# RWKV-6 attention and a SiLU expert on one core: the first three units in a written order instead of a merged one

## The chip, the cores and the metric

The kernel runs on one core of one Trainium2 chip. The metric is device time in microseconds. Before the change three runs took 745.05, 746.13 and 749.16 us; the median is 746.13.

## The reference

For 4 sequences, 8 heads, 768 steps and 48 channels a head, the attention keeps a 48x48 state for each head:

```python
for t in range(S):
    cur = np.einsum('bhd,bhe->bhde', u[None] * kt, vt)
    y[:, :, t] = np.einsum('bhd,bhde->bhe', rt, state + cur)
    state = wt[:, :, :, None] * state + np.einsum('bhd,bhe->bhde', kt, vt)
...
x = attn_out.transpose(0, 2, 1, 3).reshape(B * S, H * D)
h = x @ w_in
out = ((h * (1.0 / (1.0 + np.exp(-h)))) @ w_out).astype(np.float32)
```

r, k, v, w and u are float32. w_in (384x2048) and w_out (2048x384) are float64, so the kernel must also turn the weights into float32.

## The kernel before

**Units.** The work is cut into 12 units: 6 chunks of 128 steps times 2 pairs of sequences. In a unit, `b` is 0 or 1 for the sequence of the pair; the second one is stored in reversed order of time. Heads lie in pairs: 4 pairs (NP) for each sequence, 8 (Q) in all, and a head takes 64 partitions, 48 of them filled.

**Attention of a unit.** `turn` (L287) brings w, r and k from tokens-on-partitions to channels-on-partitions. In units 0 and 1 (NTOK) this is done by TensorE (L307) with an evacuation by ScalarE (L308); from unit 2 on the data comes in blocks of 32 (`load_blocks`, L89, four DMAs each) and VectorE transposes it (L298). Then seven levels follow (`level`, L353). In level l, blocks of 2^l steps are joined in pairs: ScalarE copies the untouched half of the keys for the next level (L365), TensorE forms scores of the later block's queries against the earlier block's keys (L377, 16 recorded matmuls), VectorE keeps the ones that belong to this level under a mask (L386, two instructions), VectorE multiplies the later queries by a product of w (L395), and POOL multiplies half of the keys (L414, two instructions). The level products of w come from POOL (L322): unit 0 makes one in each level, later units all seven at once (`products`). Unit 0 multiplies the queries before it keeps the scores; later units keep first.

`bonus` (L331) makes r·k·u for the diagonal on POOL (L333, L334), `bonus_sum` (L336) sums it on VectorE (L340) and copies the second sequence's part on ScalarE (L343), `bonus_write` (L345) writes it into the diagonal of the scores (L347, L349). `reverse_v` (L315) reverses the values of the second sequence in place (L317). `y_state` and `y` (L437, L445) form the output of the unit on TensorE, `dense_x` (units 0 and 1, L483) or `move_x` (DMAs, L495) packs it into xt; `turn_k` (L422) and `update` (L459, L475) carry the state on. `clear` (L313) zeroes padding of a raw buffer before blocks are loaded into it.

**Keys.** The tile `tk` has 16 rows of 128 for each partition. Rows 0 to 7 hold the keys of the unit, rows 8 to 11 and 12 to 15 the keys that even and odd levels read (`x_at`). The key products of L414 write in one instruction both into the keys and into the rows that the next level reads, with a step between them.

**Expert.** `up(i, m)` (L549) multiplies two 128-column blocks of w_in with the unit's xt and ScalarE applies Silu (L552) into a `gt` buffer; there are eight `up` in a unit. `down` (unit 0, L559, eight parts) and `quarter` (later units, L604, seven quarters, a scheme with seven products in place of eight) multiply with w_out. The quarters need `sums` of gt (L586) and `weight_sums` of w_out (L578), made by VectorE.

**Weights.** They come as 16 pieces. `load_weight` (L151) brings the 64-bit words of a piece into a staging place, either one of three `own` places or a part of w_out_sb that isn't filled yet; `PLACES` says which, and a place that was used before is loaded again only after the earlier piece is joined (`due`). `round_weight(i)` (L203) issues the addition of what is joined so far (POOL, L201), joins piece i-1 (VectorE, L189 and L191, each twice), splits piece i (VectorE L169; ScalarE L173 twice, L175) and issues the loads that are now due. The buffers `temps` hold two pieces, so a split waits for the addition of the piece two before it. The tails of a split lie in the two `p_o` banks.

**Order.** Every engine runs its instructions in the order in which the program issues them. `mix(i)` gives a unit's attention steps with shares, `merge` (L634) sorts several lists of steps by shares over given stretches and issues them. Units 0 to 2 are one merge of 12 lists (L652); from unit 3 on a unit's attention is merged with `quarter`s of unit i-2 and `up`s of unit i-1 (L657). Set-up (L214 to L279) comes ahead of all: memsets on VectorE, the identity, masks and the diagonal mask `own_mask` on POOL, the first loads on SP.

Of the kernel before, what the change touches and what calls it, by code (L numbers as in the profile page):

```python
# [33 lines left out]
def kernel(  # L34
# [11 lines left out]
    nc = tc.nc  # L46
# [9 lines left out]
    NX = Q + 2 * NP  # L56
    TU = NB * L
# [74 lines left out]
    PLACES = [3, 4, 5, 6, 0, 1, 2, 3, 4, 5, 6, 0, 1, 2, 6, 0]  # L132
# [81 lines left out]
    for s in range(NSLOT):  # L214
        nc.vector.memset(raw[:, s].rearrange("p x b h d -> p (x b h) d")[:, :, D:PD], 0.0)
# [22 lines left out]
    nc.vector.memset(state, 0.0)  # L238
# [36 lines left out]
    own_mask = const.tile([128, NB, L], I8, name="own_mask")  # L275
    nc.gpsimd.memset(own_mask, 1)
    for b, sign in ((0, 1), (1, -1)):
        nc.gpsimd.affine_select(out=own_mask[:, b], in_=own_mask[:, b], compare_op=ALU.is_equal, fill=0.0,
                                base=-b * (L - 1), pattern=[[1, L]], channel_multiplier=-sign)  # L279


# [5 lines left out]
    def turn(i, b, name):  # L287
        dst = {"w": tw, "r": tr, "k": tk}[name]
        if b == 0:
            rows = NX if name == "k" else Q  # L290
            t = pt.tile([128, rows, L], F32, name="t" + name, bufs=1)
            dst[i] = [t] if name == "w" else t
        t = dst[i][0] if name == "w" else dst[i]
        to, back = t[:, b * NP:(b + 1) * NP, :], name == "k" and b == 1
        if i < NTOK:
            turn_all(i, b, name, to, back)
        else:
            nc.vector.transpose(out=to[:, ::-1, ::-1] if back else to,  # L298
                                in_=raw[:, i % NSLOT, WRK[name], b].rearrange("p h d -> p (h d)"))
# [9 lines left out]

    def clear(i):  # L310

        room = raw[:, i % NSLOT].rearrange("p x b h d -> p (x b h d)").rearrange("p (g d) -> p g d", d=32)[:, :, D - 32:32]
        nc.scalar.copy(out=room, in_=zero[:, :, None].to_broadcast([128, room.shape[1], room.shape[2]]))  # L313
# [17 lines left out]
    def bonus(i, b):  # L331
        ruk[i, b] = pt.tile([128, H, D], F32, name="ruk")
        nc.gpsimd.tensor_tensor(out=ruk[i, b], in0=rk(i, b, 0), in1=rk(i, b, 1), op=ALU.mult)  # L333
        nc.gpsimd.tensor_tensor(out=ruk[i, b], in0=ruk[i, b], in1=u_bc, op=ALU.mult)  # L334

    def bonus_sum(i, b):  # L336
        if b == 0:
            diag[i] = pt.tile([128, NB, H], F32, name="diag", bufs=2)
        to = pt.tile([128, H], F32, name="diag_b") if b == 1 else diag[i][:, 0]
        nc.vector.tensor_reduce(out=to, in_=ruk[i, b], axis=mybir.AxisListType.X, op=ALU.add)  # L340
        if b == 1:
            for g in range(4):
                nc.scalar.copy(out=diag[i][(3 - g) * 32:(4 - g) * 32, 1], in_=to[g * 32:(g + 1) * 32])  # L343
# [9 lines left out]
    def level(i, l):  # L353
# [3 lines left out]
        x_at, next_at = Q + l % 2 * NP, Q + (l + 1) % 2 * NP  # L357
# [5 lines left out]
        if l + 1 < NL:  # L363

            nc.scalar.copy(out=keys(next_at * L + c, [4 * c, NP * ni // 2], [c, 2], [1, c]),  # L365
                           in_=keys(c, [4 * c, NP * ni // 2], [NP * L + c, 2], [1, c]))
# [33 lines left out]
        for b in range(NB):  # L400
            if l + 1 < NL:
                start = [next_at * L, b * NP * L][b] + b * c
                step = 2 * c + (1 - 2 * b) * (b * NP - next_at) * L
# [3 lines left out]
            else:  # L407
                out = keys(b * NP * L + b * c, [L, NP], [1, c])
# [93 lines left out]
    def mix(i):  # L502

        steps = []
        for name in ("krw", "wrk")[i] if i < NTOK else "wkr":

            steps += [((1, 0.3)[i] if i < NTOK else 0, turn, i, b, name) for b in range(NB)]
            if name == "w" and i > 0:
                steps.append((0, products, i))
        if i >= NTOK:  # L510
            steps.append((TURNS, lambda: None))
        steps.append((0, reverse_v, i))
        for l in range(NL):
# [7 lines left out]
        turns = [(1 if i > 0 else 0.3, turn_k, i, b) for b in range(NB)]  # L521
        ys = [(0, y_state, i, b) for b in range(NB)] + [(0, y, i, b) for b in range(NB)]
        updates = [(0, update, i, b) for b in range(NB)]
        if i < NTOK:
            steps += ys + [(0, dense_x, i, b) for b in range(NB)] + turns + updates
        else:
            steps += turns + ys + updates + [(1, move_x, i)]

        last = [at for at, step in enumerate(steps) if step[1] is (bonus if i < NTOK else turn)][-1] + 1
        loads = block_loads(i + NSLOT) if NTOK <= i and i + NSLOT < len(units) else []  # L530
        if 2 <= i + 1 < len(units):
# [6 lines left out]
        steps = spread  # L538
        return steps


    gt, po = {}, {}

    def up(i, m):
# [6 lines left out]
        gt[i, m] = pt.tile([128, 2, TU], F32, name="gt", bufs=FC // 2 + 3)  # L551
# [94 lines left out]
    def early_blocks(i):  # L646
        return [(1, *step) for step in [(clear, i - NSLOT)] + [step[1:] for step in block_loads(i)]]
# [40 lines left out]
```

## Time and profile before

| What | Value |
|---|---|
| median of the three runs | 746.13 us |
| the profiled execution's own time | 745.98 us |
| its span, from first to last instruction | 744.3 us |
| PE busy | 681.8 us (92%) |
| DVE (VectorE) busy | 441.1 us (59%) |
| POOL busy | 270.9 us (36%) |
| ACT (ScalarE) busy | 174.7 us (23%) |
| mean granted TensorE clock | 0.956 |

In the page's slices each digit is the busy share of one fortieth of the span, 18.6 us, in tenths, and PEclk is the granted TensorE clock in tenths of full speed. In the table by stretches, each engine has its busy microseconds and the number of instructions, then follow the granted clock, the share of time in which the DMA engines were busy, and GB/s. A row of the timeline has start, duration, engine, line, operation, output and inputs, and in brackets how long the engine had been idle and what ended that. PEld is the loading of matmul weights, which overlaps PE. SPq and ACTq are DMA issues. Rows of DMA issues give the number, the size and the median time from issue to landing.

### The profile page before, as it was taken

The page shows a single profiled execution, that of the slowest core. Times are in us where ns is not written, and L with a number is a line of the kernel's source. Part 1 is how long each engine was busy: PE and PEld are TensorE (multiplying, and loading weights), DVE is VectorE, ACT ScalarE, POOL GpSimd, SP SyncE. Part 2 cuts the span into 40 slices and gives each one's busy share as a digit, 9 for nine tenths or more (in the row PEclk, how much of TensorE's full clock was granted, in tenths as well). Part 3 has the DMA queues.
Part 4 walks back from the last instruction along what each step waited for, and adds up shares of the span by engine and source line. Part 5 has one row for each costly group of instructions (what it writes and reads, how often), then busy time and mean ns, then how long its engine had stood idle before and what let it go on. Part 6 is the DMA issues. An engine that isn't in the chain of part 4 may idle for free.

```text
span 744.3 us, 12848 instructions
## 1 busy us (share of the span) xinstructions
PE 681.8 (92%) x4880; PEld 598.5 (80%) x4880; DVE 441.1 (59%) x783; ACT 174.7 (23%) x366; POOL 270.9 (36%) x376
## 2 busy tenths in 40 slices
PE   4584788399999999999999999999999999999998
PEld 3573666257988988988988988988988988988998
DVE  3746695977556656646646646756746747645122
ACT  4243444601202213112112113113112123022020
POOL 8725744570361351441442432431431441330000
PEclk9586789799999999999999999999999999999999
DMA  9904760554225234234144143143143020100000
GB/s 209 268 2 107 167 151 10 110 82 80 44 45 89 39 64 71 39 73 66 33 80 60 33 86 55 34 86 57 29 91 57 19 64 15 41 11 20 24 1 22
DMA packets 224239, 49.04 MB, mean 66 GB/s; under 512 B 212017, under 2 KB 219057, under 8 KB 224177
## 3 DMA queue, kind: packets, MB, share of 16 engines
q1 hardware_dynamic: 224032, 48.02, 33.5%
q8 instruction: 39, 0.64, 0.4%
q10 hardware_dynamic: 144, 0.20, 0.1%
q14 instruction: 24, 0.19, 0.1%
HBM read 39.52 MB, written 4.72 MB: 59 GB/s over the span
## 4 chain that ended last, share of the span: by engine, by line
PE 81%; DVE 9%; POOL 3%; ACT 2%; SPq 2%; issue 2%; DMA 1%; DVEq 0%; POOLq 0%
PE p_h L549 34%; PE p_o L604 24%; PE p_sc L377 11%; DVE score L386 4%; PE p_m L437 3%; PE p_m L445 3%; PE p_o L559 3%; DVE tr L395 2%; POOL tk L414 1%; DVE temps L191 1%; PE p_sc L459 1%; DVE p_o L189 1%; POOL w_in_sb L201 1%; ACT kq L424 1%; PE p_m L483 1%
## 5 line engine op out<-in xcount | busy, mean ns | idle before, releaser
L549 PE MATMUL p_h<-xt,w_in_sb 128*128 128x256 f32 x1152 | 276.7, 395 | 16.1 <-POOL w_in_sb L201 16.1
L549 PEld LDWEIGHTS p_h<-xt,w_in_sb 128*128 128x128 f32 x1152 | 220.8, 196 | 52.1 <-POOL w_in_sb L201 17.1
L386 DVE COPY_PREDICATED score<-mask,p_sc 128x512 f32<-128x512 int8 x162 | 133.4, 889 | 130.5 <-PE p_sc L377 130.5
L414 POOL TENSOR_TENSOR tk<-tk,tw 128x256 f32<-128x256 f32 x168 | 119.0, 730 | 213.1 <-PE p_sc L377 114.4
L552 ACT ACTIVATE gt<-p_h 128x512 f32<-128x512 f32 x96 | 57.1, 595 | 284.2 <-PE p_h L549 284.1
L377 PEld LDWEIGHTS p_sc<-tr,tk 48*128 48x128 f32 x1296 | 84.4, 197 | 48.3 <-issue 25.0
L377 PE MATMUL p_sc<-tr,tk 48*128 48x128 f32 x1296 | 100.2, 296 | 22.2 <-POOL tk L414 12.4
L604 PE MATMUL p_o<-w_out_sb,gt 128*128 128x192 f32 x528 | 90.3, 328 | 0.0
L604 PE MATMUL p_o<-own,temps 128*128 128x192 f32 x528 | 90.0, 328 | 0.0
L604 PEld LDWEIGHTS p_o<-w_out_sb,gt 128*128 128x128 f32 x528 | 86.2, 190 | 1.7
L604 PEld LDWEIGHTS p_o<-own,temps 128*128 128x128 f32 x528 | 85.9, 190 | 1.1
L395 DVE TENSOR_TENSOR tr<-tr,tw 128x512 f32<-128x512 f32 x82 | 65.7, 801 | 3.9 <-POOL ruk L333 2.2
L322 POOL TENSOR_TENSOR tw<-tw 128x512 f32<-128x512 f32 (+6 forms) x84 | 39.4, 468 | 75.3 <-DVE tw L298 66.8
L365 ACT COPY tk<-tk 128x256 f32<-128x256 f32 x72 | 32.7, 454 | 129.8 <-POOL tk L414 85.9
L464 POOL TENSOR_TENSOR state<-state,tw 128x512 f32<-128x512 f32 x16 | 16.3, 1041 | 87.8 <-PE p_m L437 87.8
L586 DVE TENSOR_TENSOR temps<-gt 128x256 f32<-128x256 f32 x88 | 36.9, 419 | 15.6 <-ACT gt L552 15.3
L613 DVE TENSOR_TENSOR ob<-p_o,partial 128x192 f32<-128x192 f32 x44 | 15.5, 352 | 39.5 <-PE p_o L604 39.4
L349 DVE COPY_PREDICATED score<-own_mask,diag 128x1024 f32<-128x1024 int8 x24 | 31.3, 1360 | 0.4
L604 PE MATMUL p_o<-w_out_sb,temps 128*128 128x192 f32 x176 | 31.3, 331 | 0.0
L604 PEld LDWEIGHTS p_o<-w_out_sb,temps 128*128 128x128 f32 x176 | 28.4, 190 | 1.1
L473 DVE TENSOR_TENSOR state<-p_sc,state 48x384 f32<-48x384 f32 x16 | 8.9, 555 | 32.9 <-PE p_sc L459 32.8
L334 POOL TENSOR_TENSOR ruk<-ruk,u_bc 128x384 f32<-128x384 f32 x24 | 26.0, 1081 | 1.9
(83 smaller groups left out, 563.5 us busy)
## 6 DMA issues: line engine op xcount, KB each, us to landing
out_dram<-ob SPq DMA_DIRECT2D x24, 192.0 KB, 1.9
w_out_sb<-in_moe_w_in_dram SPq DMA_DIRECT2D x5, 768.0 KB, 7.0
tokens_rk<-in_r_dram SPq DMA_DIRECT2D x10, 384.0 KB, 4.1
tokens_rk<-in_k_dram SPq DMA_DIRECT2D x10, 384.0 KB, 5.4
w_out_sb<-in_moe_w_out_dram SPq DMA_DIRECT2D x4, 768.0 KB, 4.9
own<-in_moe_w_out_dram SPq DMA_DIRECT2D x4, 768.0 KB, 5.2
xt<-yt SPq DMA_DIRECT2D x60, 48.0 KB, 2.0
raw<-in_w_dram SPq DMA_DIRECT2D x80, 32.0 KB, 2.2
```

The costliest lines, as they stand in the source:

```text
L322: nc.gpsimd.tensor_tensor(out=up, in0=t[:, :, 0::2], in1=t[:, :, 1::2], op=ALU.mult)
L334: nc.gpsimd.tensor_tensor(out=ruk[i, b], in0=ruk[i, b], in1=u_bc, op=ALU.mult)
L349: nc.vector.copy_predicated(out=score[:, i % NSC, e].rearrange("p (b q) t -> p b q t", b=NB), mask=own_mask[:, :, None, :].to_broadcast([1 ...
L365: nc.scalar.copy(out=keys(next_at * L + c, [4 * c, NP * ni // 2], [c, 2], [1, c]), in_=keys(c, [4 * c, NP * ni // 2], [NP * L + c, 2], [1, ...
L377: nc.tensor.matmul(bass.AP(tensor=s_p.tensor, offset=s_p.offset, ap=[s_p.ap[0], [apart * L // 2, 2], [1, L // 2]]), lhsT=tk[i][rows, x_at ...
L386: nc.vector.copy_predicated(out=dst, mask=masks[l][:, :, None].to_broadcast([128, NB, NP, ni, c]), data=sc[e].rearrange("p (b q) (i c) -> ...
L395: nc.vector.tensor_tensor(out=rb[:, :, :, 1, :], in0=rb[:, :, :, 1, :], in1=t[:, :, 0::2][:, :, :, None].to_broadcast([128, Q, ni, c]), op ...
L414: nc.gpsimd.tensor_tensor(out=out, in0=have, in1=odd, op=ALU.mult)
L549: nc.tensor.matmul(p_h[:, a, :], lhsT=w_in_sb[:, c, f * 128:(f + 1) * 128], rhs=xt[i][:, c, :], start=(c == 0), stop=(c == KC - 1))
L552: nc.scalar.activation(out=gt[i, m], in_=p_h, func=AF.Silu)
L586: nc.vector.tensor_tensor(out=out, in0=one, in1=two, op=op)
L604: nc.tensor.matmul(p, lhsT=left(f), rhs=right[:, f, :], start=(f == 0), stop=(f == FH - 1))
```

## The change

- **Order of units 0 to 2.** The merge of 12 lists goes; a written list takes its place. Unit 0 begins with the whole bonus. Its values are reversed after level 3, and piece 0 of the weights is split there. Between the levels of unit 0 and of unit 1 stand pieces 1, 2 and 3, between the steps of y, dense_x and the turns. In unit 1 each level is followed by one piece (4 to 10) and one `up` of unit 0. Pieces 11 and 12 stand around dense_x of unit 1, 13 to 17 (16 only joins, 17 only adds) before the levels of unit 2 with `up` 0 to 4 of unit 1. The levels of unit 2 have between them `up` 5 to 7 of unit 1 and `down` of unit 0.
- **Key layout.** Rows 0 to 3 and 12 to 15 are now what even and odd levels read, the keys are rows 4 to 11.
- **First bonus.** In unit 0 the products and the four small copies of the bonus run on VectorE.
- **Products of w.** Unit 1 makes them one in each level, as unit 0 does.
- **Staging.** The third `own` place is not used for weights; three `gt` buffers of unit 0 lie there. Six pieces are loaded at the start, not seven.
- **Set-up.** The state and the padding of the second raw buffer are zeroed by ScalarE among unit 0's levels, not by VectorE ahead of them; `own_mask` is made before the other masks.
- `mix` loses its cases for units 0 and 1; for units 3 to 11 it gives the steps it gave.

```diff
+    X = 0, NP + Q
...
-    PLACES = [3, 4, 5, 6, 0, 1, 2, 3, 4, 5, 6, 0, 1, 2, 6, 0]
+    PLACES = [3, 4, 5, 6, 0, 1, 3, 4, 5, 6, 0, 1, 5, 0, 6, 1]
...
-    for s in range(NSLOT):
-        nc.vector.memset(raw[:, s].rearrange("p x b h d -> p (x b h) d")[:, :, D:PD], 0.0)
+    nc.vector.memset(raw[:, 0].rearrange("p x b h d -> p (x b h) d")[:, :, D:PD], 0.0)
...
-    nc.vector.memset(state, 0.0)
...
+    def clear_all(room):
+        nc.scalar.copy(out=room, in_=zero[:, :, None].to_broadcast(list(room.shape)))
...
+    def clear_state():
+        clear_all(state.rearrange("p b q d -> p (b q) d"))
+
+    def clear_tokens():
+        clear_all(raw[:, 1].rearrange("p x b h d -> p (x b h) d")[:, :, D:PD])
...
     def bonus(i, b):
+        engine = nc.gpsimd if i > 0 else nc.vector
         ruk[i, b] = pt.tile([128, H, D], F32, name="ruk")
-        nc.gpsimd.tensor_tensor(out=ruk[i, b], in0=rk(i, b, 0), in1=rk(i, b, 1), op=ALU.mult)
-        nc.gpsimd.tensor_tensor(out=ruk[i, b], in0=ruk[i, b], in1=u_bc, op=ALU.mult)
+        engine.tensor_tensor(out=ruk[i, b], in0=rk(i, b, 0), in1=rk(i, b, 1), op=ALU.mult)
+        engine.tensor_tensor(out=ruk[i, b], in0=ruk[i, b], in1=u_bc, op=ALU.mult)
...
+            copy = nc.scalar.copy if i > 0 else nc.vector.tensor_copy
             for g in range(4):
-                nc.scalar.copy(out=diag[i][(3 - g) * 32:(4 - g) * 32, 1], in_=to[g * 32:(g + 1) * 32])
+                copy(out=diag[i][(3 - g) * 32:(4 - g) * 32, 1], in_=to[g * 32:(g + 1) * 32])
...
-        x_at, next_at = Q + l % 2 * NP, Q + (l + 1) % 2 * NP
+        x_at, next_at = X[l % 2], X[(l + 1) % 2]
...
+            row0 = NP + b * NP
             if l + 1 < NL:
-                start = [next_at * L, b * NP * L][b] + b * c
-                step = 2 * c + (1 - 2 * b) * (b * NP - next_at) * L
+                start = [next_at * L, row0 * L][b] + b * c
+                step = 2 * c + (1 - 2 * b) * (row0 - next_at) * L
...
-        if alone:
+        if i < NTOK:
             product(i, l)
         add_weight()
...
+        if i == 0 and m < NFIRST:
+            gt[i, m] = own[:, NOWN - 1, m * 2 * TU:(m + 1) * 2 * TU].bitcast(F32).rearrange("p (a t) -> p a t", a=2)
+        else:
+            gt[i, m] = pt.tile([128, 2, TU], F32, name="gt", bufs=FC // 2 + 3)
...
-    weights = [(1, round_weight, i) for i in range(2 * NW + 2)]
-    merge((mix(0), 0.0, 1.0), (mix(1), 0.95, 2.0), (mix(2), 2.0, 3.0),
-          (weights[:1], 0.6, 0.7), (weights[1:NW + 1], 1.0, 1.83), (weights[NW + 1:], 1.85, 2.4),
-          (early_blocks(2), 1.02, 1.7), (early_blocks(3), 2.02, 2.6),
-          (ups(0), 1.12, 1.95), (ups(1)[:3], 2.0, 2.4), (downs(0), 2.4, 2.75), (ups(1)[3:], 2.75, 3.0),
-          ([(1, weight_sums, x) for x in range(3)], 2.45, 2.75), ([(1, weight_sums, 3)], 2.8, 2.85))
+    do(*both(bonus, 0), *both(bonus_sum, 0), (bonus_write, 0),
+       *both(turn, 0, "k"), *both(turn, 0, "r"), *both(turn, 0, "w"), (level, 0, 0), (clear_state,), (level, 0, 1),
+       (level, 0, 2), (level, 0, 3), (reverse_v, 0), (round_weight, 0), (level, 0, 4), (clear_tokens,), (level, 0, 5),
+       (level, 0, 6))
+    do(*both(turn, 1, "w"), *both(turn, 1, "r"), *both(y_state, 0), *both(y, 0), (round_weight, 1), *both(dense_x, 0),
+       (round_weight, 2), *both(turn_k, 0), *both(turn, 1, "k"), (reverse_v, 1), (round_weight, 3))
+    loads = [(clear, 0)] + [step[1:] for step in block_loads(2)]
+    others = {0: both(update, 0), 1: [(bonus, 1, 0)], 2: [(bonus, 1, 1)], 3: [(bonus_sum, 1, 0)], 4: [(bonus_sum, 1, 1)],
+              5: [(bonus_write, 1)], 6: [(load_rk, 2), (load_values, 2)]}
+    for l in range(NL):
+        do((level, 1, l), (round_weight, 4 + l), (up, 0, l), *others[l], *loads[l * 2:l * 2 + 2])
+    do((up, 0, 7), *both(y_state, 1), *both(y, 1), (round_weight, 11), *both(dense_x, 1), (round_weight, 12),
+       *both(turn_k, 1), *both(turn, 2, "w"), (products, 2), *both(update, 1), (clear, 1))
+    loads = [step[1:] for step in block_loads(3)]
+    turns = {0: both(turn, 2, "k"), 1: both(turn, 2, "r"), 2: [(reverse_v, 2)]}
+    for m in range(5):
+        do((round_weight, 13 + m), (up, 1, m), *turns.get(m, ()), *loads[m * 3:m * 3 + 3])
+    work = [[(up, 1, 5), (sums, 1, 0)], [(down, 0, 0, 0), (down, 0, 0, 1)], [(down, 0, 0, 2), (down, 0, 0, 3)],
+            [(down, 0, 1, 0), (down, 0, 1, 1)], [(down, 0, 1, 2), (down, 0, 1, 3)], [(up, 1, 6)], [(up, 1, 7)]]
+    others = {1: [(bonus, 2, 0), (weight_sums, 0)], 2: [(bonus, 2, 1), (load_rk, 3), (weight_sums, 1)],
+              3: [(bonus_sum, 2, 0), (sums, 1, 1)], 4: [(bonus_sum, 2, 1), (weight_sums, 2)],
+              5: [(weight_sums, 3), (bonus_write, 2)], 6: [(sums, 1, 2), (load_values, 3)]}
+    loads = [step[1:] for step in block_loads(4)]
+    for l in range(NL):
+        do((level, 2, l), *work[l], *others.get(l, ()), *loads[l * 2:l * 2 + 2])
+    do(*both(turn_k, 2), *both(y_state, 2), *both(y, 2), *both(update, 2), (move_x, 2))
```

`do` issues the steps in the order given; `both` gives a step for b = 0 and b = 1.

More of the change, by code (lines that the diff above doesn't have):

```diff
@@ L250 @@
                                in_=ident[rows, PD * e + d0:PD * e + d1])
+    own_mask = const.tile([128, NB, L], I8, name="own_mask")
+    nc.gpsimd.memset(own_mask, 1)
+    for b, sign in ((0, 1), (1, -1)):
+        nc.gpsimd.affine_select(out=own_mask[:, b], in_=own_mask[:, b], compare_op=ALU.is_equal, fill=0.0,
+                                base=-b * (L - 1), pattern=[[1, L]], channel_multiplier=-sign)
     masks = []
@@ L272 @@
         nc.vector.memset(score[:, s], 0.0)
[L275 to L279, printed above, removed]
     tw, tr, tk, diag, kq, xt = {}, {}, {}, {}, {}, {}
@@ L293, in turn @@
         t = dst[i][0] if name == "w" else dst[i]
-        to, back = t[:, b * NP:(b + 1) * NP, :], name == "k" and b == 1
+        row0 = b * NP + (NP if name == "k" else 0)
+        to, back = t[:, row0:row0 + NP, :], name == "k" and b == 1
         if i < NTOK:
@@ L504, in mix @@
         steps = []
-        for name in ("krw", "wrk")[i] if i < NTOK else "wkr":
-            steps += [((1, 0.3)[i] if i < NTOK else 0, turn, i, b, name) for b in range(NB)]
-            if name == "w" and i > 0:
+        for name in "wkr":
+            steps += [(0, turn, i, b, name) for b in range(NB)]
+            if name == "w":
                 steps.append((0, products, i))
-        if i >= NTOK:
-            steps.append((TURNS, lambda: None))
-        steps.append((0, reverse_v, i))
+        last = len(steps)
+        steps += [(TURNS, lambda: None), (0, reverse_v, i)]
         for l in range(NL):
-            steps.append((LEVEL + (i >= NTOK and l < 2), level, i, l))
+            steps.append((LEVEL + (l < 2), level, i, l))
             if l in (1, 2):
                 steps.append((0, bonus, i, l - 1))
+            if l == 2 and i + 1 < len(units):
+                steps.append((0, load_rk, i + 1))
             if l in (3, 4):
@@ L520, in mix @@
                 steps.append((0, bonus_write, i))
[L521 to L531, printed above, removed]
+        steps += [(1, turn_k, i, b) for b in range(NB)]
+        steps += [(0, y_state, i, b) for b in range(NB)] + [(0, y, i, b) for b in range(NB)]
+        steps += [(0, update, i, b) for b in range(NB)] + [(1, move_x, i)]
+        loads = block_loads(i + NSLOT) if i + NSLOT < len(units) else []
+        if i + 1 < len(units):
             loads.insert(len(loads) // 2, (0, load_values, i + 1))
-        if NTOK <= i + 1 < len(units):
-            steps.insert([at for at, step in enumerate(steps) if step[1] is bonus][-1] + 1, (0, load_rk, i + 1))
         spread, room = steps[:last], len(steps) - last
@@ L537, in mix @@
             spread += [steps[last + at], *loads[at * len(loads) // room:(at + 1) * len(loads) // room]]
-        steps = spread
-        return steps
+        return spread
     gt, po = {}, {}
+    NFIRST = 2 * PW // (2 * TU)
     def up(i, m):
@@ L644, with do @@
     NU = len(units)
[L646 to L656 removed]
+    def do(*steps):
+        for fn, *args in steps:
+            fn(*args)
@@ new lines, in both @@
+    def both(fn, i, *args):
+        return [(fn, i, b, *args) for b in range(NB)]
+    do(*both(bonus, 0), *both(bonus_sum, 0), (bonus_write, 0),
[4 more added lines that the diff above has]
+       (round_weight, 2), *both(turn_k, 0), *both(turn, 1, "k"), (reverse_v, 1), (round_weight, 3))
```

12 lines of the change are left out of this document (5 added, 7 removed).

## The prediction

> **What bounds the kernel now.** I read the page first (its 40 slices), then busy time by stage, then the timeline of the first 156 us.
>
> ```profile
> PE   4584788399999999999999999999999999999998
> PEclk9586789799999999999999999999999999999999
> ```
> ```profile
> core 0: us, PE busy (x) PEld busy (x) DVE busy (x) ACT busy (x) POOL busy (x), PEclk, DMA share, GB/s
> 17.60:38.80 21.20, 12.43 (x97) 10.86 (x97) 17.22 (x25) 4.08 (x11) 15.05 (x22) 0.51 1.00 243
> 38.80:54.60 15.80, 13.44 (x138) 11.85 (x136) 5.42 (x10) 7.44 (x15) 3.02 (x7) 0.90 0.01 2
> 54.60:107.50 52.90, 36.80 (x197) 28.66 (x197) 40.40 (x63) 23.21 (x42) 30.45 (x26) 0.74 0.65 150
> 122.00:152.30 30.30, 15.73 (x74) 11.58 (x74) 28.56 (x43) 14.31 (x24) 20.07 (x19) 0.80 0.40 80
> 152.30:195.40 43.10, 43.10 (x286) 32.11 (x287) 28.11 (x42) 6.51 (x15) 13.71 (x16) 1.00 0.46 74
> ```
> From 152.3 us on TensorE never pauses and its clock is full: nothing that the change does to the other engines shortens that. Before it TensorE has holes and a lowered clock. The stages are: set-up and the tokens' arrival, unit 0's levels, the passage to unit 1 (VectorE at 5.4 of 15.8 us: room), unit 1's levels with weight pieces 1 to 8 between them, and the start of unit 2 (VectorE at 28.6 of 30.3). The forecast is therefore: at what time does the first stage without holes begin, and how much TensorE work is then left?
>
> The profiled execution took 745.98 us, 1.7 more than its span, and the median is 746.13. I work in span time and take the difference off 746.0.
>
> **Unit 0.** Now:
> ```profile
> 1.30 1.31 SPq L86 DMA_DIRECT2D raw<-in_r_dram  x1
> 13.78 0.54 POOL L278 TENSOR_SCALAR_AFFINE_SELECT own_mask<-own_mask 128x128 int8<-128x128 int8 x2
> 14.74 1.63 POOL L414 TENSOR_TENSOR tk<-tk,tw 128x256 f32<-128x256 f32 x2 [0.42 <-PE p_sc L377]
> 17.12 0.01 DVE L317 LOAD_MASK_SELECT vq<-vq  x1 [9.13 <-DMA vq<-in_v_dram]
> 17.63 1.09 DVE L395 TENSOR_TENSOR tr<-tr,tw 128x512 f32<-128x512 f32 x1
> 21.05 1.43 DVE L395 TENSOR_TENSOR tr<-tr,tw 128x512 f32<-128x512 f32 x1
> 22.40 2.42 DVE L386 COPY_PREDICATED score<-mask,p_h 128x512 f32<-128x512 int8 x2
> 33.52 1.31 DVE L386 COPY_PREDICATED score<-mask,p_sc 128x512 f32<-128x512 int8 x2
> 35.92 0.69 DVE L395 TENSOR_TENSOR tr<-tr,tw 128x512 f32<-128x512 f32 x1 [0.66 <-issue]
> 36.76 2.08 PE L377 MATMUL p_sc<-tr,tk 48*128 48x128 f32 x16 [0.93 <-DVE tr L395]
> 37.96 2.50 DVE L349 COPY_PREDICATED score<-own_mask,diag 128x1024 f32<-128x1024 int8 x2
> ```
> ```profile
> raw<-in_r_dram SPq DMA_DIRECT2D x1, 384.0 KB, 6.9
> 54.31 0.55 DVE L191 SCALAR_TENSOR_TENSOR temps<-w_out_sb,p_o 128x384 uint32<-128x384 uint32 x1
> 54.48 1.47 ACT L313 COPY raw<-zero 128x1536 f32<-128x1536 f32 x1
> ```
> VectorE stands 9.1 us before the values' reversal, which waits for v, with the first query product (17.63) behind it. The change puts the reversal after level 3, where v has long landed (17.1), and fills the wait with the first bonus. Its start: r was issued at 1.3 and landed 6.9 later, at 8.2. Its length: four 128x384 products at 0.55 (nearest row L191, same size, two inputs) make 2.2; two sums over as many columns 1.1; four 32x8 copies, for which no VectorE row exists, between 0.2 and 0.8, the middle 0.5; shuffle of 8 columns 0.2; diagonal 2.50 (L349). So VectorE is free at 8.2 + 6.5 = 14.7, and the first query product ends at 15.8. The two memsets that go to ScalarE come before 8.2 on VectorE and save nothing there; on ScalarE, by L313's 1.47 for 1536 elements, they cost 2.0 (2048) and 0.7 (768), in queue gaps of unit 0's levels (ScalarE 4.1 of 21.2 busy): nothing; uncovered, 2.7.
>
> POOL's masks still end at 14.3 (the same instructions in another order), so its first key products end at 14.35 + 1.63 = 16.0, and the second score product runs 16.1 to 18.2. The query product of level 1 takes 1.43 and 0.14 of issue, the next score product 2.08 (ends 21.95), while the kept scores take VectorE 2.42 until 22.1. From there a level is query product 0.69 + issue 0.14 + score product 2.08 + 0.1 = 3.0: no bonus stands on POOL or VectorE. The key products no longer wait for the score product of their level, since the keys that it reads now lie outside the span which they write. The last score product ends at 22.1 + 3 x 3.05 + 0.4 (what reversal and first split, 0.55 each, with the kept scores' 1.31 leave over 2.1) + 2.9 = 34.5, against 38.84 now: **4.3 gained**.
>
> A rule that bears here: the Trainium skill, "TensorE: Matmul & The Clock Gate", Part 1, says that the array runs at half clock until a window of about 3.4 us was busy, and falls back after an idle one. The row first: 17.6 to 38.8 was granted 0.51 throughout at a busy share of 59%. By the rule a denser stage might go warm; that is rival 3.
>
> **The passage, with three pieces.**
> ```profile
> 55.84 0.55 DVE L169 TENSOR_SCALAR temps<-w_out_sb 128x768 uint32<-128x768 uint32 x1
> 55.86 0.94 ACT L173 ACTIVATE p_o<-w_out_sb 128x384 f32<-128x384 uint16 x2
> 56.74 0.92 ACT L175 ACTIVATE temps<-temps,shift 128x768 uint32<-128x768 uint32 x1
> 58.30 2.09 POOL L414 TENSOR_TENSOR tk<-tk,tw 128x256 f32<-128x256 f32 x2 [13.37 <-ACT tk L365]
> ```
> A piece costs VectorE 4 x 0.55 to join and 0.55 to split, 2.75; ScalarE 0.94 + 0.92 = 1.86; POOL an addition of about 2. VectorE has 10 us free here, three pieces take 8.3: hidden. ScalarE queues them between the evacuations: each piece's two steps wait for VectorE, and the copies of xt, kq and tk stand behind them. Three pieces are 5.6; one piece and the clear, which now stand ahead of unit 1's first key product, are 3.3. So the stretch grows by 0 (hidden in ScalarE's idle half) to 2.3; I take 0.5, since turning r ahead of y shortens the ping-pong between TensorE and ScalarE. Unit 1's first key product goes from 58.3 to 54.5.
>
> **Unit 1's levels.**
> ```profile
> 93.06 0.58 ACT L552 ACTIVATE gt<-p_h 128x512 f32<-128x512 f32 x1
> 93.54 0.39 ACT L365 COPY tk<-tk 128x256 f32<-128x256 f32 x1
> 94.06 1.20 POOL L414 TENSOR_TENSOR tk<-tk,tw 128x256 f32<-128x256 f32 x2 [0.21 <-ACT tk L365]
> 100.59 5.49 PE L549 MATMUL p_h<-xt,w_in_sb 128*128 128x256 f32 x12 [2.73 <-POOL w_in_sb L201]
> 103.28 2.06 POOL L201 TENSOR_TENSOR w_in_sb<-temps 128x768 uint32<-128x768 uint32 x1 [1.15 <-DVE temps L191]
> 103.79 3.90 DVE L349 COPY_PREDICATED score<-own_mask,diag 128x1024 f32<-128x1024 int8 x2
> 111.99 1.08 PE L445 MATMUL p_m<-score,vt 128*48 128x128 f32 x16
> ```
> TensorE now waits for additions (2.73, then 5.49 at half clock). With three pieces ahead, `up` m finds its weights ready. What is late next is a loop through the buffers: `temps` holds two heads, so a split (L169) waits for the addition of the piece two before, which POOL makes at the end of this level, behind the key products; ScalarE's second step, the Silu and the key copy (L365) follow, and L365 releases the next key products. One turn: key products 1.4 (between 1.20 and 1.63), weight product 0.3 (unit 1's products now lie in its levels; an estimate by size, at most 128 columns against the key products' 256), addition 2.0, split 0.55, L175 0.92, Silu 0.58, L365 0.39, and some 0.4 of handoffs: 6.5. VectorE alone would need 2.75 + 1.31 + 0.69 = 4.8, so the loop binds. The first turn is longer: 2.09 + 1.0 (weight product of 512 columns, by the two key products' 2.09 for as many) + 2.06 + 0.55 + 0.92 + 0.58 + 1.47 (clear) + 0.39 + 0.5 = 9.6. The bonus on POOL beside two splits and its four ScalarE copies add 1.8. Level 5's key products start at 54.5 + 9.6 + 4 x 6.5 + 1.8 = 91.9; 3.7 later the addition is done; then split 0.55, diagonal 2.5 to 3.9, level 6 kept 1.3: y of unit 1 at 100.5 to 101.9, say 101, against 111.99: **11 gained** so far, with pieces 0 to 9 (now 0 to 8) split by then. SP's queue carries the same 48 block issues and the reloads in this stretch as it does now, and their first reader is unit 2's turn, after y: nothing.
>
> **To the start of unit 2.**
> ```profile
> 120.87 1.12 DVE L475 COPY state<-p_sc 48x384 f32<-48x384 f32 x2 [6.78 <-PE p_sc L459]
> 122.01 1.30 DVE L298 STREAM_TRANSPOSE tw<-raw 128x512 f32<-128x512 f32 x2
> 123.39 3.48 POOL L322 TENSOR_TENSOR tw<-tw 128x512 f32<-128x512 f32 x7 [10.23 <-DVE tw L298]
> 147.87 2.85 PE L559 MATMUL p_o<-w_out_sb,gt 128*128 128x384 f32 x8 [1.78 <-DVE temps L191]
> 152.30 1.16 PE L377 MATMUL p_sc<-tr,tk 48*128 48x128 f32 x16 [1.58 <-DVE tr L395]
> ```
> VectorE has rounds 10 to 15 (16.5), the last join 2.2, three turns 3.9, the state copies 1.1, a reversal 0.6, and level 0 of unit 2 (2.4 + 1.1): 27.8. To that I add 6.5 of waiting: the products of unit 2 hold POOL 3.5 us ahead of an addition (2.5), the y copies stand behind two Silus and a piece on ScalarE and release the state copies and `up` late (3), handoffs (1). With level 1's score product, 1.2 (full clock), TensorE has no hole after 101 + 27.8 + 6.5 + 1.2 = 136.5, if `up` keeps pace; five of them (2.7 each, 13.5) fit between xt at about 113 and there. After that each of levels 1 to 4 gives TensorE two parts of `down`, 5.4, more than VectorE's 4 to 6 us per level.
>
> The same place in the order (levels 0 and 1 of unit 2 done) is 152.30 now, where 3 `up` of unit 1 and one part of `down` are done. Changed, it is 6 `up` and none: 2 x 2.7 = 5.4 less remains. Sum: 152.3 - 136.5 + 5.4 = 21.2; 746.0 - 21.2 = **724.8**. The list from unit 3 on is the same.
>
> **Rivals.** 0.5% is about what a measurement of this kernel can tell from no change (745.05 to 749.16 were three runs of one kernel).
> 1. *VectorE alone binds unit 1* (the additions slip in beside VectorE's joins): 4.8 to 5 a level where I have 6.5, over six levels 10 less: 714. For it: 40.4 of 52.9 busy now; against it the buffers.
> 2. *The pieces aren't hidden.* ScalarE delays the passage by 2.3, not 0.5, and the late `up` of unit 1 run at half clock, 5.49 for 2.75, four of them: 724.8 + 1.8 + 11 = 737.
> 3. *The clock warms in unit 0*: there score products would be 68% of a 3.0 us level; at 1.16 for 2.08, six levels save 5.5: 719. Against: 36.76 is still 2.08 after such levels.
> 4. *The layout frees nothing*: key products still wait in unit 0's even levels, about 1 each: 728.
> 5. *Given back, no change (within 0.5%)*: a piece misses its data because weight 6 loses its own staging place, and the later ones reload after joins; three waits of one landing:
> ```profile
> w_out_sb<-in_moe_w_in_dram SPq DMA_DIRECT2D x5, 768.0 KB, 7.0
> ```
> 724.8 + 3 x 7.0 = 746. Against: each reload is issued two rounds or more ahead of its split, 9 us and more.
> 6. *Slower.* POOL's key products, no longer held by the score product, run against VectorE's products in all ten later units. Place: the level with one quarter of `down` between two score products:
> ```profile
> 213.95 1.16 PE L377 MATMUL p_sc<-tr,tk 48*128 48x128 f32 x16 [0.35 <-DVE tr L395]
> ```
> There the slack is already gone. A unit must lose 2.2 more to eat the 21 us, and it decides from there; 3 per unit gives 724.8 + 30 = 755. Against: the key products last as long whenever they run, and VectorE's wait there is not for POOL.
>
> **How the numbers follow.** Forecast 0.57, rival 1 0.12, rival 2 0.10, rival 3 0.07, rival 4 0.05, rival 5 0.04, rival 6 0.05. Faster 0.91, same 0.04, slower 0.05. The range takes the forecast's own bounds (2.3 in the passage, 2.7 of ScalarE clears, 5 of waits in either sense) and rivals 1 to 4: 712 to 737; outside it are rivals 5 and 6 and the edges of 1 and 2.
>
> **What would show it.** Unit 0's last score product ends near 34.5; the first query product starts near 14.7; unit 1's key products start near 54.5 and then every 6 to 7 us, with L169 waiting for L201; y of unit 1 near 101; no `up` waits for w_in_sb; TensorE without holes from about 136. Wrong if unit 1's period is near 5 (rival 1), if `up` still shows 5.49 (rival 2), or if the units after 200 us have become longer (rival 6).

## The result and the profile after

The changed kernel took 729.58 us (median of four runs, 728.50 to 730.68), beside 747.64 us for the kernel before on the same chips (745.05 to 749.39). The ratio is 0.976, with a 95% interval of 0.972 to 0.980: faster. 724.8 us was predicted, 712 to 737 as the range. The profiled execution took 730.68 us with a span of 729.0, so between the two profiled executions the span fell by 15.3 us. The kernel before lies in two groups (two of its four runs near 745.5, two near 749.3) and had medians of 745.1 to 745.7 beside the experiments below; against those the change is worth some 16 us, not 18.

The page of the changed kernel, its slices for TensorE and for the granted clock, and then busy time by stage (the ends have moved with the work, except 54.6, which is kept although unit 1's first score product started at 54.63 before and starts at 53.05 now; the third stage ends here at y of unit 1):

```profile
PE   3688777998999999999999999999999999999998
PEclk9588998999999999999999999999999999999999
```
```profile
core 0: us, PE busy (x) PEld busy (x) DVE busy (x) ACT busy (x) POOL busy (x), PEclk, DMA share, GB/s
17.60:37.30 19.70, 12.46 (x97) 10.91 (x97) 12.84 (x19) 4.37 (x9) 13.50 (x22) 0.50 0.98 223
37.30:54.60 17.30, 14.01 (x121) 12.13 (x120) 9.49 (x19) 12.23 (x24) 4.06 (x2) 0.89 0.42 134
54.60:98.90 44.30, 36.60 (x246) 29.67 (x242) 40.44 (x60) 19.02 (x36) 31.28 (x32) 0.90 0.43 98
98.90:135.50 36.60, 28.32 (x201) 23.64 (x200) 25.91 (x50) 20.84 (x37) 18.59 (x17) 0.91 0.62 126
135.50:175.60 40.10, 38.03 (x258) 26.45 (x256) 27.88 (x39) 5.74 (x14) 16.91 (x18) 1.00 0.48 76
```

TensorE has no long hole after the eighth slice. Unit 1's levels up to its y (54.6 to 98.9) took 44.3 us at a granted clock of 0.90; before they took 57.4 (54.6 to 112.0) and the clock was 0.76. ScalarE's busy time in the passage rose from 7.4 to 12.2 us: the three pieces. The last row shows a place that the forecast left out: 38.0 busy of 40.1 us, where TensorE was to have no hole.

Where the gain came from and where it went, at the same events in both traces:

| Event | before | after | gain so far | forecast |
|---|---|---|---|---|
| unit 0's last score product ends | 38.84 | 37.32 | 1.5 | 4.3 |
| unit 1's first key products start | 58.30 | 55.38 | 2.9 | 3.8 |
| y of unit 1 starts | 111.99 | 98.87 | 13.1 | 11 |
| levels 0 and 1 of unit 2 done (less the 5.4 us that remain) | 152.30 | 135.5 | 22.2 | 21.2 |
| first quarter of unit 1's product with w_out | 195.22 | 175.61 | 19.6 | 21.2 |
| end of the span | 744.3 | 729.0 | 15.3 | 21.2 |

So the start gained about what was forecast, but by other amounts at its stages, which happen to add up; and 6.9 us were given back later: 2.6 in unit 2 and 4.3 in the units behind it.

### The profile page after: what moved, and what is told of

The parts are those of the page before. It is cut to its first block, busy times and chain, and to the rows that moved or that the text cites. A ratio compares the mean times of both kernels' runs of the same rounds, so it can differ in the third digit from the quotient of the medians.

```text
span 729.0 us, 12839 instructions
## 1 busy us (share of the span) xinstructions
PE 676.4 (93%) x4880; PEld 594.6 (82%) x4880; DVE 445.1 (61%) x789; ACT 174.8 (24%) x364; POOL 270.2 (37%) x372
## 4 chain that ended last, share of the span: by engine, by line
PE 79%; DVE 9%; POOL 5%; ACT 3%; DMA 2%; issue 2%; SPq 0%; POOLq 0%; ACTq 0%
PE p_h L555 32%; PE p_o L613 25%; PE p_sc L388 12%; DVE score L397 4%; PE p_m L449 3%; PE p_o L568 3%; PE p_m L457 3%; DVE tr L406 2%; POOL tk L426 1%; DMA tokens_rk<-in_k_dram 1%; POOL mask L268 1%; POOL mask L270 1%; DMA own<-in_moe_w_out_dram 1%; ACT gt L561 1%; ACT kq L436 1%
## 5 line engine op out<-in xcount | busy, mean ns | idle before, releaser
L555 PE MATMUL p_h<-xt,w_in_sb 128*128 128x256 f32 x1152 | 272.8, 392 | 4.0 <-ACT gt L561 4.0
L561 ACT ACTIVATE gt<-p_h 128x512 f32<-128x512 f32 x93 | 55.2, 594 | 272.3 <-PE p_h L555 272.3
L388 PEld LDWEIGHTS p_sc<-tr,tk 48*128 48x128 f32 x1296 | 82.6, 192 | 46.1 <-issue 25.4
L388 PE MATMUL p_sc<-tr,tk 48*128 48x128 f32 x1296 | 98.3, 291 | 21.1 <-DVE tr L406 10.9
L406 DVE TENSOR_TENSOR tr<-tr,tw 128x512 f32<-128x512 f32 x82 | 70.7, 863 | 5.9 <-issue 3.4
L595 DVE TENSOR_TENSOR temps<-gt 128x256 f32<-128x256 f32 x88 | 37.5, 426 | 15.6 <-ACT gt L561 15.3
L344 POOL TENSOR_TENSOR ruk<-ruk,u_bc 128x384 f32<-128x384 f32 x22 | 28.6, 1298 | 1.7
```

The lines of the kernel that those rows point to most:

```text
L344: engine.tensor_tensor(out=ruk[i, b], in0=ruk[i, b], in1=u_bc, op=ALU.mult)
L388: nc.tensor.matmul(bass.AP(tensor=s_p.tensor, offset=s_p.offset, ap=[s_p.ap[0], [apart * L // 2, 2], [1, L // 2]]), lhsT=tk[i][rows, x_at ...
L406: nc.vector.tensor_tensor(out=rb[:, :, :, 1, :], in0=rb[:, :, :, 1, :], in1=t[:, :, 0::2][:, :, :, None].to_broadcast([128, Q, ni, c]), op ...
L555: nc.tensor.matmul(p_h[:, a, :], lhsT=w_in_sb[:, c, f * 128:(f + 1) * 128], rhs=xt[i][:, c, :], start=(c == 0), stop=(c == KC - 1))
L561: nc.scalar.activation(out=gt[i, m], in_=p_h, func=AF.Silu)
L595: nc.vector.tensor_tensor(out=out, in0=one, in1=two, op=op)
```

## The experiments

All of them change the new kernel (one changes the kernel before) and were timed beside the kernel before. The changed kernel's own 729.58 us is from other executions, so a difference of one or two microseconds against it is read together with the trace.

**Where the units from 3 on lose.** Rows of the changed kernel's timeline in one later unit, level 1 of its attention: POOL's second bonus product, VectorE's query product and TensorE's next score product.

```profile
248.29 1.02 POOL L343 TENSOR_TENSOR ruk<-tokens_rk 128x384 f32<-128x384 f32 x1
248.70 1.17 DVE L406 TENSOR_TENSOR tr<-tr,tw 128x512 f32<-128x512 f32 x1
250.01 1.16 PE L388 MATMUL p_sc<-tr,tk 48*128 48x128 f32 x16 [0.81 <-DVE tr L406]
```

The same query product in the kernel before:

```profile
213.09 0.71 DVE L395 TENSOR_TENSOR tr<-tr,tw 128x512 f32<-128x512 f32 x1
```

The query product takes 1.17 us beside POOL's product; before the change it took 0.71 there, with POOL idle, and TensorE waited 0.35. The first run puts the old layout back:

```diff
-    X = 0, NP + Q
+    X = Q, Q + NP
...
-            row0 = NP + b * NP
+            row0 = b * NP
...
```

> The changed kernel with the old key layout alone put back. Theory A: in the later units the new layout lets POOL run ahead by a level, so that its bonus product falls beside VectorE's query product of level 1 (1.17 us for 0.71), and a unit takes 54.87 us for 54.41. Then a unit is back at 54.4 and nine of them give back 4 us; unit 0 loses 0 to 3 where the key products wait for a score product again: 726 to 729. Rival B: the later units are longer for another reason (another phase of loads and stores after the new list): a unit stays at 54.87 and the time is 730 to 733, since only the loss in unit 0 is left.

It took 726.02 us (725.38 to 726.90; ratio 0.973, 0.970 to 0.976). TensorE's wait in two later units in a row:

```profile
193.41 1.16 PE L388 MATMUL p_sc<-tr,tk 48*128 48x128 f32 x16 [0.36 <-DVE tr L406]
247.83 1.16 PE L388 MATMUL p_sc<-tr,tk 48*128 48x128 f32 x16 [0.36 <-DVE tr L406]
```

A unit is 54.42 us again (247.83 - 193.41) and the wait 0.36: theory A. The opposite run gives the kernel before the new layout and nothing else (the same lines, the other way round).

> The kernel before with the new key layout alone. Theory A: its units from 3 on go from 54.41 to 54.87 us, 4 us in all; units 0 and 1 win back 0 to 3 at the even levels: 748 to 752. Rival B: the layout costs nothing in later units, which stay at 54.41, and the time is 744 to 747.

It took 746.30 us (ratio 1.0005, 0.9989 to 1.0021). By the time alone that is rival B's range; the trace shows theory A's longer units, and why the time is below its range:

```profile
147.28 1.16 PE L379 MATMUL p_sc<-tr,tk 48*128 48x128 f32 x16 [1.60 <-DVE tr L397]
...
211.09 1.16 PE L379 MATMUL p_sc<-tr,tk 48*128 48x128 f32 x16 [0.81 <-DVE tr L397]
265.97 1.16 PE L379 MATMUL p_sc<-tr,tk 48*128 48x128 f32 x16 [0.81 <-DVE tr L397]
```

The first row is at 152.30 in the kernel before: 5.0 us won up to there, more than the 0 to 3 of theory A. At the start of unit 3 the lead is 3.3 us (199.79 for 203.12); from there a unit takes 54.88 (265.97 - 211.09) and the wait is 0.81: the win is paid back in full. The length of a later unit thus goes with the layout and not with the order of the first units: 54.41 and 54.42 us with the old layout, 54.87 and 54.88 with the new one, in the old and in the written order. The third run keeps the new layout and moves POOL's second bonus instead:

```diff
-            if l in (1, 2):
-                steps.append((0, bonus, i, l - 1))
-            if l == 2 and i + 1 < len(units):
+            if l in (1, 3):
+                steps.append((0, bonus, i, l // 2))
+            if l == 3 and i + 1 < len(units):
```

> The changed kernel, new key layout everywhere, with the second bonus of units 3 to 11 (and the load behind it) moved from behind level 2 to behind level 3. Theory A: it is POOL's second bonus product beside VectorE's query product of level 1 that costs the later units 0.46 us each. Then that query product is back at 0.7, TensorE waits 0.35 instead of 0.81 there, a unit takes 54.4 and the time is 725 to 727. Rival B: the key products themselves, or something other than this bonus, slow VectorE: units stay at 54.87 and the time at 729 to 730.

It took 725.48 us (724.68 to 726.77; ratio 0.973, 0.971 to 0.975), and the same place reads:

```profile
248.25 0.73 DVE L406 TENSOR_TENSOR tr<-tr,tw 128x512 f32<-128x512 f32 x1
249.12 1.16 PE L388 MATMUL p_sc<-tr,tk 48*128 48x128 f32 x16 [0.37 <-DVE tr L406]
```

Theory A again, and now with its cause: the new layout lets POOL go one level ahead, and the bonus product that follows falls beside the one query product that TensorE waits for. The Trainium skill ("GPSIMD Engine Reference", section 1) says that POOL's SBUF interface is shared with VectorE and contended by VectorE instructions with two SBUF inputs; the query product is one, and 1.17 against 0.73 us agrees.

**Unit 0.** Rows of the changed kernel: the diagonal on VectorE, two of POOL's masks beside it, the first key products, and the score products of levels 1 and 6.

```profile
12.86 2.54 DVE L360 COPY_PREDICATED score<-own_mask,diag 128x1024 f32<-128x1024 int8 x2
12.87 1.38 POOL L268 TENSOR_SCALAR_AFFINE_SELECT mask<-mask 128x64 int8<-128x64 int8 x1
14.32 1.15 POOL L270 TENSOR_SCALAR_AFFINE_SELECT mask<-mask 128x64 int8<-128x64 int8 x1
17.66 1.64 POOL L426 TENSOR_TENSOR tk<-tk,tw 128x256 f32<-128x256 f32 x2
19.35 2.08 PE L388 MATMUL p_h<-tr,tk 48*128 48x128 f32 x16 [5.58 <-POOL tk L426]
35.24 2.08 PE L388 MATMUL p_sc<-tr,tk 48*128 48x128 f32 x16 [1.29 <-POOL tw L330]
```

VectorE was free of the bonus at 15.3, near the forecast (14.7), but POOL's masks, which take 0.24 us of their own, took 1.38 and 1.15 beside it. The first key products start at 17.66, not at 14.35.

```diff
-    do(*both(bonus, 0), *both(bonus_sum, 0), (bonus_write, 0),
+    do(*both(bonus, 0), *both(bonus_sum, 0),
...
-       (level, 0, 6))
+       (bonus_write, 0), (level, 0, 6))
```

> The changed kernel, with the first diagonal write (and its shuffle) moved from ahead of level 0 to behind level 5. Theory A: VectorE's two diagonal copies (2.5 us) are what stretches POOL's masks from 0.24 to 1.38 us, so that the first key products start at 17.66. Moved, they start between 14.5 and 15.7, unit 0's last score product ends at about 35.3 instead of 37.3, and the time falls by 1.5 to 2.5, to about 727.5. Rival B: the bonus products or another engine's traffic stretch the masks: the first key products still start after 17 and the time stays at 729 to 730. Rival C: the start comes earlier, but the passage to unit 1 is bound by ScalarE and the pieces: 729.

It took 727.28 us (727.02 to 728.85; ratio 0.975, 0.972 to 0.978).

```profile
13.14 0.24 POOL L268 TENSOR_SCALAR_AFFINE_SELECT mask<-mask 128x64 int8<-128x64 int8 x1
15.44 1.64 POOL L426 TENSOR_TENSOR tk<-tk,tw 128x256 f32<-128x256 f32 x2
33.02 2.08 PE L388 MATMUL p_sc<-tr,tk 48*128 48x128 f32 x16 [1.28 <-POOL tw L330]
```

Theory A: the mask is back at 0.24, and the last score product ends at 35.1, 2.2 earlier. The other 1.1 us of the delay (15.44 for 14.35) are masks beside VectorE's bonus and query products, which took 0.45 to 0.75 us in this run. Two more runs ask what the other two moves in unit 0 are worth. The first puts the whole bonus back (on POOL and between the levels), the second only the reversal ahead of level 0.

```diff
-        engine = nc.gpsimd if i > 0 else nc.vector
+        engine = nc.gpsimd
...
```

> The changed kernel with the first bonus put back: on POOL behind levels 1 and 2, its sums behind levels 3 and 4, the diagonal behind level 5, four copies on ScalarE. Theory A: most of what the first bonus on VectorE gains ahead of level 0 is lost to the stretched masks. Then the masks end at about 14.4, the first key products start there and not at 17.66, four POOL products of 1 us come back between the key products, and unit 0's last score product ends between 35.5 and 37.5, as it does now (37.3): 728 to 730. Rival B: the bonus on VectorE is worth its 4 us of POOL: the last score product ends at 39 and the time is 731 to 734.

```diff
-       *both(turn, 0, "k"), *both(turn, 0, "r"), *both(turn, 0, "w"), (level, 0, 0), (clear_state,), (level, 0, 1),
+       *both(turn, 0, "k"), *both(turn, 0, "r"), *both(turn, 0, "w"), (reverse_v, 0), (level, 0, 0), (clear_state,), (level, 0, 1),
-       (level, 0, 2), (level, 0, 3), (reverse_v, 0), (round_weight, 0), (level, 0, 4), (clear_tokens,), (level, 0, 5),
+       (level, 0, 2), (level, 0, 3), (round_weight, 0), (level, 0, 4), (clear_tokens,), (level, 0, 5),
```

> The changed kernel with the reversal of unit 0's values back ahead of level 0, behind the bonus. Theory A: the move took a wait off VectorE that another one has replaced: the stretched masks hold the first key products until 17.66, later than the values land (17.1), so that the score product of level 1 starts at 19.3 either way: 729 to 730. Rival B: the reversal's wait is worth its 3 us: the score product of level 1 starts after 20.5 and the time is 731.5 to 733.

They took 728.34 us (ratio 0.977, 0.975 to 0.979) and 728.83 us (0.978, 0.976 to 0.980): theory A in both, the second 0.2 us below its range. With the bonus on POOL:

```profile
14.69 1.64 POOL L426 TENSOR_TENSOR tk<-tk,tw 128x256 f32<-128x256 f32 x2
34.31 2.08 PE L388 MATMUL p_sc<-tr,tk 48*128 48x128 f32 x16 [1.29 <-ACT tk L376]
```

With the reversal first:

```profile
17.45 0.01 DVE L325 LOAD_MASK_SELECT vq<-vq  x1 [1.81 <-DMA vq<-in_v_dram]
19.27 2.08 PE L388 MATMUL p_h<-tr,tk 48*128 48x128 f32 x16 [4.39 <-DVE tr L406]
```

As the change places it, the bonus on VectorE is worth nothing that these runs can tell: it takes POOL's four products away and gives them back as longer masks. With the diagonal behind level 5 in both, it is worth about 1 us: the last score product ends at 35.1 with the products on VectorE and at 36.4 with them on POOL. The reversal's wait is there again, but the score product of level 1 starts at 19.27 (19.35 in the changed kernel).

**The three pieces.** They go from the passage into unit 1's first levels:

```diff
-    do(*both(turn, 1, "w"), *both(turn, 1, "r"), *both(y_state, 0), *both(y, 0), (round_weight, 1), *both(dense_x, 0),
-       (round_weight, 2), *both(turn_k, 0), *both(turn, 1, "k"), (reverse_v, 1), (round_weight, 3))
+    do(*both(turn, 1, "w"), *both(turn, 1, "r"), *both(y_state, 0), *both(y, 0), *both(dense_x, 0),
+       *both(turn_k, 0), *both(turn, 1, "k"), (reverse_v, 1))
...
-        do((level, 1, l), (round_weight, 4 + l), (up, 0, l), *others[l], *loads[l * 2:l * 2 + 2])
+        do((level, 1, l), *[(round_weight, r) for r in ([2 * l + 1, 2 * l + 2] if l < 3 else [4 + l])], (up, 0, l), *others[l], *loads[l * 2:l * 2 + 2])
```

> The changed kernel with pieces 1, 2 and 3 moved from between units 0 and 1 into unit 1's first levels (two pieces in each of levels 0 to 2, then one in each). Theory A: the three pieces are hidden between the units, and a piece inside the levels costs a turn of the loop split, ScalarE, key copy, key products, addition: first key product of unit 1 about 2 earlier, y of unit 1 10 to 16 later than 98.9, the time 738 to 745. Rival B: the pieces are as well hidden in the levels: 728 to 732.

It took 739.88 us (738.96 to 740.70; ratio 0.992, 0.991 to 0.994).

```profile
108.86 1.08 PE L457 MATMUL p_m<-score,vt 128*48 128x128 f32 x16
```

Unit 1's first key products started at 51.7, 3.6 us earlier, and its y 10.0 later than 98.87: without the pieces ahead the stretch between them took 57.1 us, not 43.5. Theory A: this one move is about 10 us of the gain.

**The reload of piece 13.** Rows of the changed kernel: SP's issues, and who waits.

```profile
101.06 3.32 SPq L116 DMA_DIRECT2D tokens_rk<-in_k_dram  x1
...
110.53 1.70 SPq L156 DMA_DIRECT2D own<-in_moe_w_out_dram  x2
116.77 0.56 DVE L170 TENSOR_SCALAR temps<-own 128x768 uint32<-128x768 uint32 x1 [3.61 <-DMA own<-in_moe_w_out_dram]
119.13 10.96 PE L555 MATMUL p_h<-xt,w_in_sb 128*128 128x256 f32 x36 [4.01 <-ACT gt L561]
```

Piece 10 was joined by 102.6, which frees the place for piece 13, but the issues of the next unit's k, values and r stand ahead on SP's queue until 110.4. The price is more than the wait: the three `up` behind it took 10.96 us, 2.7 more than three of 2.75, with a granted clock of 0.50 from 119.1 to 123.0. The wait is not the same in every run: in five others that leave these issues as they are VectorE waited 1.4 to 2.8 us, and in the four of them where TensorE waited 1.3 to 2.2 us the `up` behind the wait took 2.86.

```diff
-              5: [(bonus_write, 1)], 6: [(load_rk, 2), (load_values, 2)]}
+              5: [(bonus_write, 1)], 6: []}
...
     do((up, 0, 7), *both(y_state, 1), *both(y, 1), (round_weight, 11), *both(dense_x, 1), (round_weight, 12),
+       (load_rk, 2), (load_values, 2),
```

> The changed kernel, with the issues of the next unit's r, k and values (7 transfers) moved from level 6 of unit 1 to behind piece 12. Theory A: these issues hold SP's queue from 100.5 to 108 us, the reload for piece 13 stands behind them (issued 110.5) and lands at 116.7, where VectorE waits 3.6 and TensorE 4.0 us for it. Moved, it is issued at about 106, lands by 112, the two waits go, and the time falls by 3 to 4, to about 726. Rival B: the transfers themselves are the bound, the reload lands as late as before, or unit 2's bonus now waits for its r and k: 729 to 731.

It took 726.27 us (725.71 to 726.74; ratio 0.973, 0.970 to 0.976).

```profile
102.72 3.84 SPq L156 DMA_DIRECT2D own<-in_moe_w_out_dram  x2
113.32 0.55 DVE L170 TENSOR_SCALAR temps<-own 128x768 uint32<-128x768 uint32 x1
130.11 1.18 PE L388 MATMUL p_sc<-tr,tk 48*128 48x128 f32 x16 [0.39 <-DVE tr L406]
```

Theory A: VectorE's wait is gone, and level 1's score product of unit 2 starts at 130.11, not at 134.40.

**Together, and unit 2.** The diagonal behind level 5, the late issues, and the new layout for units 0 and 1 alone:

```diff
-    X = 0, NP + Q
+    def X(i):
+        return (0, NP + Q) if i < NTOK else (Q, Q + NP)
...
```

> The changed kernel with three edits together: the diagonal write behind level 5, the next unit's issues behind piece 12, and the new key layout for units 0 and 1 only (old from unit 2 on). If the three losses are separate places on the path, their gains add up: 2.3 + 3.3 + 4.1 below 729.6, 719 to 722. If two of them are the same slack (an earlier start only lengthens the wait for the reload), 722 to 725.

It took 720.40 us (719.94 to 721.38; ratio 0.966, 0.964 to 0.968): the three add up, to 9.2 of 9.7. The same with the old layout everywhere:

> The kernel of the three mended places with the old key layout in every unit. Theory A: in the written order the new layout is worth little in units 0 and 1 (with the old one, unit 0 of the changed kernel lost 0.6 us at one even level): 720.5 to 722. Rival B: with the masks' stretch gone, POOL is on the path of unit 0 and the even levels cost about 1 us each, three of them: 723 to 724.

It took 721.52 us (ratio 0.968, 0.966 to 0.970): theory A; the new layout is worth about 1 us in units 0 and 1, where y of unit 1 starts 1.1 us later without it (97.73 and 96.60), though the two intervals overlap. What was left in unit 2 was two waits of TensorE for VectorE; in the changed kernel they read

```profile
164.97 1.16 PE L388 MATMUL p_sc<-tr,tk 48*128 48x128 f32 x16 [0.81 <-DVE tr L406]
...
171.06 2.02 PE L449 MATMUL p_m<-tr,state 128*128 128x128 f32 x16 [1.26 <-DVE tr L406]
```

```diff
-              3: [(bonus_sum, 2, 0), (sums, 1, 1)], 4: [(bonus_sum, 2, 1), (weight_sums, 2)],
-              5: [(weight_sums, 3), (bonus_write, 2)], 6: [(sums, 1, 2), (load_values, 3)]}
+              3: [(bonus_sum, 2, 0), (sums, 1, 1), (weight_sums, 2)], 4: [(bonus_sum, 2, 1)],
+              5: [(bonus_write, 2)], 6: [(weight_sums, 3), (sums, 1, 2), (load_values, 3)]}
```

> The kernel of the three mended places, with unit 2's third sum of weights issued one level earlier (ahead of the last parts of the product with w_out) and its fourth one level later (behind the diagonal). Theory A: these two VectorE steps, 1.75 us each, stand ahead of the kept scores of levels 5 and 6 and cause TensorE's two waits in unit 2 (0.80 and 1.26 us). Then both go and the time falls by 1.5 to 2 against the three mended places, to 718.5 to 719. Rival B: the diagonal alone (2.5 us) holds VectorE long enough: the second wait stays at 0.8 or more, and the time stays within 1 us of 720.4.

It took 718.76 us (718.13 to 718.88; ratio 0.964, 0.962 to 0.966; the interval overlaps that of the three mended places, so the two waits decide): theory A. The first wait isn't in the trace any more, the second is 0.29:

```profile
162.49 2.05 PE L454 MATMUL p_m<-tr,state 128*128 128x128 f32 x16 [0.29 <-ACT kq L441]
```

This is the fastest version, 10.8 us under the changed kernel.

## Why the prediction was right, and where its steps failed

The sign, the stage from which most of the gain comes and the time to within 5 us were right; of 21.2 us of gain the spans show 15.3. Part of that is luck: against its own terms unit 0 gave 2.8 us less, the passage 1.9 more, unit 1's levels 3.0 more and the way to unit 2 1.1 less, and only their sum comes out (22.2 for 21.2). The three signs by which the prediction was to be known as wrong also showed: a period near 5 in unit 1, longer units after 200 us and, once, behind the reload of piece 13, an `up` of 5.49. The steps:

- *Unit 0, 4.3 gained*: failed; 1.5. The failed sentence is "POOL's masks still end at 14.3 (the same instructions in another order)": the order put them beside VectorE's diagonal, which the trace of before has after the masks' end. Moving the diagonal gave 2.2 of it back. VectorE's own sum (free at 14.7; measured 15.3) held, but POOL, not VectorE, set the start of the key products. The levels behind it held: from the end of level 2's score product to that of level 6 they took 12.75 us, for 12.6 in the sum.
- *The passage grows by 0.5*: wrong in both parts, small in sum. From the last score product to the first key products it shrank by 1.4 us (19.5 to 18.1). Without the pieces it was 14.9 (51.7 - 36.9), so they cost 3.2, where I had counted 5.6 of ScalarE; all else (the turns' order, piece 1 and the clear no longer ahead of the first key copy) won 4.6, where I had counted 5.1.
- *Unit 1's loop, 6.5 a turn*: its first turn held (9.1 for 9.6), the later ones took 5.2 on the mean (from 64.44 to 90.66 in five), so the loop as counted did not bind them. Rows of the changed kernel:

```profile
71.88 1.29 POOL L426 TENSOR_TENSOR tk<-tk,tw 128x256 f32<-128x256 f32 x2 [0.96 <-ACT tk L376]
75.34 1.34 DVE L170 TENSOR_SCALAR temps<-w_out_sb 128x768 uint32<-128x768 uint32 x1 [1.36 <-POOL w_in_sb L202]
77.51 1.68 POOL L426 TENSOR_TENSOR tk<-tk,tw 128x256 f32<-128x256 f32 x2
78.04 0.39 ACT L376 COPY tk<-tk 128x256 f32<-128x256 f32 x1
```

  The split does wait for the addition (1.36), but level 3's key products (77.51) start ahead of that level's key copy (78.04), and so do those of levels 4 and 5: the last link of the loop isn't one there. In level 2 (the first row) they do wait for it. VectorE was busy 40.4 of 44.3 us, so the stage is near rival 1, VectorE alone (4.8 to 5 a level), and y came 2 us before the forecast.
- *To the start of unit 2, 35.5 us*: 36.6 measured, but the 6.5 of waiting in it were of other kinds than I listed: 3.6 is the reload of piece 13. Rival 5's mechanism was real, once instead of three times, and behind SP's queue, whose issues I had put at nothing in the stage before. Rival 2 as it was meant didn't come true (the passage shrank), though its sign, an `up` at half clock, showed once behind the reload.
- *"The list from unit 3 on is the same"*, and no loss in unit 2: failed; 6.9. The list was the same, but the key layout holds for these units too, and with it POOL comes a level earlier. Rival 6 named the place and the cause (POOL's freed work beside VectorE's products, at the short level), but through the bonus and not the key products, and at 0.46 a unit instead of 3. In unit 2 I compared VectorE and TensorE for levels 1 to 4 and left out levels 5 and 6, where TensorE has less work than VectorE.
- *Rival 3* didn't come true: unit 0's levels were granted 0.50 at a busy share of 63%. The Trainium skill ("TensorE: Matmul & The Clock Gate", Part 1) gives the full clock only after a busy window of about 3.4 us; such a share, then, did not make one, and the trace does not show which share would.
- *Rival 4*, that the layout frees nothing, was half right: about 1 us in this order, though 3 to 5 us in the order before.

The step that carried most of the gain, pieces ahead of the levels that would have to wait for them, held: about 10 of some 16 us.

What stays open: how much of unit 1's stage is VectorE's own work and how much the waits for additions; no run took the second buffer of `temps` away or added a third. No run tests the order of the turns, unit 1's products of w, the staging or the clears by themselves.

## What to carry to other kernels

A step moved to an idle engine is also moved beside something on its neighbours: read what the other engines run in that window, since an operation's time from a quiet stretch is not its time there. A wait that is taken away for the head's sake is gone in the steady state too where both share the code; this steady state was balanced to a few tenths of a microsecond, and there each tenth counts once a unit. And a queue that is free on average can still hold the one transfer that is due: list what is issued ahead of it.

## What the runs showed of the hardware

- POOL's mask selects of 0.24 us took 1.38 and 1.15 us beside VectorE's predicated copy with mask and data in SBUF, and 0.24 with that copy moved away; beside the predicated copies that read scores from PSUM (15.93 to 18.35 in the changed kernel) they stayed at 0.24.
- VectorE's query product of two SBUF inputs took 1.17 us beside POOL's product and 0.73 alone: the stretch goes both ways.
- SP spent 3.32 us issuing one transfer of 384 KB (k), and 0.47 on another of that size (r) just ahead of it; the issues behind follow with gaps of 0.1 us, so the reload was held by issue time. Why the one took so much longer no run shows.
- Behind a wait of 4.0 us TensorE's granted clock was 0.50 in the next 3.9 us and an `up` took 5.49 us; behind waits of 1.3 to 2.2 us, in four other runs, it took 2.86.
